# A SwiGLU kernel whose first 128 tokens of x are loaded by two queues, 64 rows each

## The chip, the cores and the metric

The kernel runs on one core of one Trainium2 chip. The metric is the device time of one execution in microseconds (us). Five engines of the core take part, each with its own queue of instructions that it works off in order: TensorE (PE in the profile, with its weight loads listed apart as PEld), VectorE (DVE), ScalarE (ACT), GpSimd (POOL) and SyncE (SP). SyncE and ScalarE also issue DMAs; a DMA issued on SyncE is told as queue q1 in the profile, one issued on ScalarE as q10. They meet through semaphores: a DMA adds 16 to its semaphore when all of its data has landed, and an engine that needs the data waits for that count.

## The reference

The kernel computes a feed-forward block with a SiLU gate, on x of 1 x 2048 x 512, with a hidden width F of 1376, all in bfloat16:

```python
def reference(x, w_gate, w_up, w_down):
    g = _silu(x @ w_gate)     # x: 2048 x 512, w_gate: 512 x 1376
    u = x @ w_up              # w_up: 512 x 1376
    return (g * u) @ w_down   # w_down: 1376 x 512
```

## The kernel before

**Tiling.** The 2048 tokens are worked in four chunks of 512 (`SC`), F in ten full tiles of 128 and a rest of 96. The inner dimension 512 is cut in `KD` = 4 pieces of 128. For chunk c and tile ft a group G (gate) and a group U (up) each run four matmuls of 128 x 128 weights against x transposed (`xT_sb`), and leave their result in one of eight PSUM banks. ScalarE applies SiLU to G, VectorE multiplies with U into `hT_sb`. When all of that is done the second half of the kernel multiplies `hT_sb` with `w_down` and stores the rows.

**How x gets transposed.** From the third tile of 128 tokens on, DMAs do it (`load_x`, line 93). The first two tiles (`NXN` = 2) come in untransposed by plain DMAs into `xn_sb` (`load_xn`, line 113; tile i has the semaphore `xn0` or `xn1`), and TensorE transposes them: `transposes(i)` (line 362) waits for the tile's load and then does four transposing matmuls, one for each dk, against the identity `ident`. Each leaves one 128 x 128 block in a bank; VectorE copies blocks dk = 0 and 2 to `xT_sb`, ScalarE dk = 1 and 3 (the loop at line 214). The matmuls of G and U wait for the copy that they read (`gu_step`, line 339).

**The order at the start, on each queue.**
- SyncE (`loads_on_sync`, line 123) issues in this order: xn0; the up weights of tile 0 (semaphore `wu0`); gate and up weights of tile 1 (`wg1`, `wu1`); gate and up weights of tiles 2 and 3 (`wg2`, `wu2`, twice as large); the transposing loads x0b and x0c of tokens 256 to 511; then the other weights, the other chunks of x, and `w_down`.
- ScalarE (`loads_on_scalar`, line 119) issues the gate weights of tile 0 (`wg0`) and then xn1. After that come the load of its function table and a small SiLU on a constant (line 277), and then its copies out of the banks.
- TensorE (from line 358) runs `N_WARM` = 5 matmuls of 512 columns and `N_FILL` = 2 of 128 on constants; then transposes(0), which waits for xn0; two more constant matmuls (`N_GAP`); G of tile 0 on tokens 0 to 127, which waits for `wg0` and for the copies; transposes(1), which waits for xn1; U of tile 0 on tokens 0 to 127, which waits for `wu0`; both groups on tokens 128 to 255; then, on tokens 0 to 255, G and U of tile 1 (`wg1`, `wu1`), G of tiles 2 and 3 (`wg2`), U of tiles 2 and 3 (`wu2`); then the same groups on the other half of the chunk (x0b, x0c). From there every group runs whole, 512 columns wide.

All waits for loads on TensorE go through `need(name, count)` (line 306), which waits until the semaphore is at 16 times the count.

Of the kernel before, what the change touches and what calls it, by code (L numbers as in the profile page):

```python
# [14 lines left out]
def bass_standalone__swiglu_ffn__prompt_kernel(nc, x, w_gate, w_up, w_down, out):  # L15
    _, S, D = x.shape
    F = w_gate.shape[1]
    P = 128
# [23 lines left out]
    xf = x[0]  # L42
# [8 lines left out]
    with ExitStack() as es:  # L51
# [19 lines left out]
        xn_sb = sb("xn_sb", [P, NXN, D], BF16)  # L71
# [10 lines left out]
        loads = {}  # L82

        def load_sem(name):
            loads[name] = sem(f"s_{name}")
            return loads[name]
# [6 lines left out]
        def load_x(eng, name, t0, t1):  # L93
            eng.dma_start_transpose(
                xT_sb[:, :, t0:t1], xf[t0:t1, :]
            ).then_inc(load_sem(name), 16)

        def load_w(eng, name, src, base, f0, f1):
            eng.dma_start(
                w_sb[:, :, base + f0:base + f1],  # L100
                src[:, f0:f1].rearrange("(k p) f -> p k f", p=P),
            ).then_inc(load_sem(name), 16)
# [4 lines left out]
        def load_gate(eng, a, b):  # L107
            load_w(eng, f"wg{a}", w_gate, 0, a * P, min(b * P, F))

        def load_up(eng, a, b):  # L110
            load_w(eng, f"wu{a}", w_up, UPH, a * P, min(b * P, F - 32))

        def load_xn(eng, i):
            eng.dma_start(xn_sb[:, i, :], xf[i * P:(i + 1) * P, :]).then_inc(load_sem(f"xn{i}"), 16)

        def out_rows(t):
            return of[t * P:(t + 1) * P, :]

        def loads_on_scalar(act):
            load_gate(act, *slabs[0])  # L120
            load_xn(act, 1)

        def loads_on_sync(sp):
            load_xn(sp, 0)
            load_up(sp, *slabs[0])
            for a, b in slabs[1:3]:
                load_gate(sp, a, b)
                load_up(sp, a, b)
            load_x(sp, "x0b", HT, HT + P)
            load_x(sp, "x0c", HT + P, SC)  # L130
            for a, b in slabs[3:]:
                load_gate(sp, a, b)
                load_up(sp, a, b)
            load_w(sp, "wut", w_up, F - (F - 32), F - 32, F)
            for c in range(1, NSC):
                load_x(sp, f"x{c}", c * SC, (c + 1) * SC)
            sp.dma_start(
                wd_sb[:, 0:NFF, :], w_down[0:NFF * P, :].rearrange("(k p) d -> p k d", p=P)
            ).then_inc(load_sem("wd"), 16)
            load_sem("wdt")  # L140
            for y0 in (0, 64):
                sp.dma_start(wd_sb[y0:y0 + 64, T01, :], w_down[NFF * P:F - SR, :]).then_inc(loads["wdt"], 16)
            for x0 in range(0, P, SR):
                sp.dma_start(wd_sb[x0:x0 + SR, T2, :], w_down[F - SR:F, :]).then_inc(loads["wdt"], 16)
            sp.dma_start(wd_sb[0:F_LAST, TAIL, :], w_down[NFF * P:F, :]).then_inc(load_sem("wdl"), 16)
# [19 lines left out]
        def tview(i, dk):  # L165
            return banks[KD * i + dk][:, 0:P // 2].bitcast(BF16)
# [47 lines left out]
        for i in range(NXN):  # L214
            for dk in range(KD):
                eng = "DA"[dk % 2]
# [16 lines left out]
        for at, t in enumerate(tiles):  # L233
            ob = at % NOS
            need = 16 * n_store[ob]
            parts = [(0, D)] if at < NST - 1 else [(0, LASTA), (LASTA, LASTB), (LASTB, D)]
            for c0, c1 in parts:
                g = add_group("O", t=t, c0=c0, c1=c1)
                eng = "A" if at % 2 == 1 and c0 == 0 else "D"
                op = add_op(  # L240
                    eng, g, kind="copy", out=o_sb[ob][:, c0:c1], src=g["bank"][:, 0:c1 - c0],
# [17 lines left out]
        def on_sync(sp):  # L259
            loads_on_sync(sp)  # L260
            store_tiles(sp, "S")
            for i in range(NOS):
                sp.wait_ge(s_out[i], 16 * n_store[i])
# [11 lines left out]
        def on_scalar(act):  # L275
            loads_on_scalar(act)
            act.activation(adummy[:, 0:4], zero_c, ACT.Silu)  # L277
            for op in act_ops:
                act.wait_ge(*ready(op))
                if op["kind"] == "silu":  # L280
                    if op["free"]:
                        act.wait_ge(s_D, op["free"])
                    fn = ACT.Silu
                else:
                    if op["stored"][1]:
                        act.wait_ge(*op["stored"])
                    fn = ACT.Copy
                act.activation(op["out"], op["src"], fn).then_inc(s_A, 1)  # L288
            store_tiles(act, "A")
# [13 lines left out]
        def on_tensor(pe):  # L303
            landed = set()

            def need(name, count=1):
                if name not in landed:
                    pe.wait_ge(loads[name], 16 * count)
                    landed.add(name)
# [50 lines left out]
            pe.wait_ge(s_I, 1)  # L360

            def transposes(i):
                need(f"xn{i}")
                for dk in range(KD):
                    pe.matmul(  # L365
                        tview(i, dk), lhsT=xn_sb[:, i, dk * P:(dk + 1) * P], rhs=ident[:, :],
                        start=True, stop=True, is_transpose=True,
                    ).then_inc(s_X, 1)

            first = groups[0:NB]  # L370
            transposes(0)
            warm(N_GAP, P)
            gu_matmuls(first[0], 0, P)
            transposes(1)
            gu_matmuls(first[1], 0, P)
            for dk in range(KD):
# [143 lines left out]
```

## Time and profile before

| | |
|---|---|
| median of 3 runs | 119.98 us (119.94 to 120.01) |
| the profiled execution's own time | 119.89 us |
| its span in the profile | 118.6 us |
| what lies around the span | 1.29 us |
| TensorE busy | 115.9 us, 98% of the span |
| VectorE / ScalarE busy | 38.0 us (32%) / 35.1 us (30%) |
| granted TensorE clock | 1.0 over the whole span |
| HBM read / written | 4.75 MB / 2.10 MB |

The span is what the profile covers, from the first instruction to the last; the time of a run has 1.29 us more in it. All times of single instructions below are counted from the span's start. A busy TensorE is not a TensorE at its peak: matmuls overlap, and their recorded ends are modelled. So for TensorE the start times of matmuls and weight loads say more than the busy time: in the stretches without a wait, a matmul with 128 columns starts every 0.056 us, one with 256 every 0.109 us and one with 512 every 0.216 us.

### The profile page before, as it was taken

Reading aid. Unit: us, or ns where it says so; the run is one execution under the profiler, and the core shown is the slowest. Engines: PE = TensorE matmul, PEld = TensorE weight load, DVE = VectorE, ACT = ScalarE, POOL = GpSimd, SP = SyncE. Lnnn points to the kernel's source line nnn. Section 1 sums busy time; section 2 is a strip of 40 time slices with the busy share of each in tenths; the row PEclk is TensorE's granted clock in tenths of the full one; section 3 lists DMA queues with packets and bytes.
Section 4 is the critical chain, followed back from the end, with each engine's and each line's share of the span. In section 5 each row is a group of like instructions: output and inputs, shape, how many; then the busy total and the mean of one; then the engine's idle time right before and its main releaser. Section 6 shows DMA issues by size and latency. Waiting matters only on the chain.

```text
span 118.6 us, 2344 instructions
## 1 busy us (share of the span) xinstructions
PE 115.9 (98%) x1019; PEld 59.7 (50%) x1019; DVE 38.0 (32%) x60; ACT 35.1 (30%) x62; POOL 1.1 (1%) x7
## 2 busy tenths in 40 slices
PE   7999999999999999999999999999999999999993
PEld 2788444444444444444444444444444445885442
DVE  0206542444433444324444244360000044003321
ACT  3407334353244272343263432330000033003021
POOL 1000000000000000000000000010000000000000
PEclk9999999999999999999999999999999999999999
DMA  3999999991000000000000000000000017200612
GB/s 87 290 186 336 296 161 221 268 357 25 0 6 0 0 0 0 0 3 3 0 0 6 0 0 0 0 0 6 0 6 0 0 57 237 70 0 6 202 64 88
DMA packets 17642, 8.83 MB, mean 74 GB/s; under 512 B 10624, under 2 KB 17632, under 8 KB 17632
## 3 DMA queue, kind: packets, MB, share of 16 engines
q1 hardware_dynamic: 16816, 8.33, 27.3%
q10 hardware_dynamic: 816, 0.36, 1.1%
q8 instruction: 8, 0.13, 0.5%
q14 instruction: 2, 0.02, 0.0%
HBM read 4.75 MB, written 2.10 MB: 58 GB/s over the span
## 4 chain that ended last, share of the span: by engine, by line
PE 98%; DVE 0%; issue 0%
PE bank L324 62%; PE bank L442 25%; PE bank L481 7%; PE bank L356 2%; PE bank L404 2%; PE bank L365 1%; DVE o_sb L300 0%
## 5 line engine op out<-in xcount | busy, mean ns | idle before, releaser
L324 PE MATMUL bank<-xT_sb,w_sb 128*128 128x512 bf16 (+2 forms) x384 | 73.3, 352 | 0.1
L324 PEld LDWEIGHTS bank<-xT_sb,w_sb 128*128 128x128 bf16 x384 | 36.2, 98 | 36.8 <-DMA w_sb<-in_w_gate_dram 0.3
L296 DVE TENSOR_TENSOR hT_sb<-sg_sb,bank 128x512 bf16<-128x512 f32 x40 | 27.5, 688 | 40.2 <-PE bank L324 39.3
L288 ACT ACTIVATE sg_sb<-bank 128x512 f32<-128x512 f32 x40 | 23.9, 597 | 40.6 <-PE bank L324 40.5
L442 PE MATMUL bank<-wd_sb,hT_sb 32*128 32x512 bf16 x496 | 29.0, 374 | 0.0
L442 PEld LDWEIGHTS bank<-wd_sb,hT_sb 32*128 32x128 bf16 x496 | 15.2, 93 | 11.6 <-issue 0.4
L300 DVE CAST o_sb<-bank 128x512 bf16<-128x512 f32 (+1 forms) x10 | 5.7, 595 | 31.1 <-PE bank L442 25.9
L288 ACT ACTIVATE o_sb<-bank 128x512 bf16<-128x512 f32 (+1 forms) x8 | 4.3, 582 | 33.6 <-PE bank L442 27.9
L481 PE MATMUL bank<-wd_sb,hT_sb 128*128 128x512 bf16 (+2 forms) x56 | 8.1, 304 | 0.0
L481 PEld LDWEIGHTS bank<-wd_sb,hT_sb 128*128 128x128 bf16 x56 | 4.2, 98 | 4.2 <-issue 0.4
L442 PE MATMUL bank<-wd_sb,hy_sb 32*128 32x512 bf16 (+1 forms) x32 | 5.0, 371 | 0.0
L296 DVE TENSOR_TENSOR hx_sb<-sgx_sb,bank 32x512 bf16<-32x512 f32 x4 | 2.8, 692 | 3.5 <-ACT sgx_sb L288 3.5
L288 ACT ACTIVATE sgx_sb<-bank 32x512 f32<-32x512 f32 x4 | 2.4, 588 | 4.5 <-PE bank L324 4.5
L356 PE MATMUL bank<-const-bfloat16-1.0 128*128 128x512 bf16 (+1 forms) x9 | 2.8, 463 | 0.8 <-PEq L505 0.8
L442 PE MATMUL bank<-wd_sb,hx_sb 32*128 32x512 bf16 (+1 forms) x16 | 3.0, 371 | 0.0
L288 ACT ACTIVATE sgy_sb<-bank 64x512 f32<-64x512 f32 x4 | 2.4, 590 | 0.1
L356 PEld LDWEIGHTS bank<-const-bfloat16-1.0 128*128 128x128 bf16 x9 | 1.0, 128 | 2.2 <-issue 2.2
L300 DVE COPY xT_sb<-bank 128x128 bf16<-128x128 bf16 x4 | 0.8, 222 | 4.3 <-PE bank L365 4.3
L404 PE MATMUL bank<-xT_sb,w_sb 128*64 128x512 bf16 x16 | 1.9, 382 | 0.0
L442 PEld LDWEIGHTS bank<-wd_sb,hy_sb 32*128 32x128 bf16 x32 | 1.6, 93 | 0.6
L277 ACT ACT_TABLE_LOAD x1 | 1.3, 1283 | 1.9 <-issue 1.9
L404 PEld LDWEIGHTS bank<-xT_sb,w_sb 128*64 128x64 bf16 x16 | 0.8, 109 | 1.0 <-DVE hT_sb L296 0.4
(15 smaller groups left out, 6.6 us busy)
## 6 DMA issues: line engine op xcount, KB each, us to landing
out_dram<-o_sb SPq DMA_DIRECT2D x15, 128.0 KB, 1.8
wd_sb<-in_w_down_dram SPq DMA_DIRECT2D x1, 1280.0 KB, 7.3
w_sb<-in_w_gate_dram SPq DMA_DIRECT2D x1, 480.0 KB, 5.5
w_sb<-in_w_up_dram SPq DMA_DIRECT2D x1, 448.0 KB, 6.2
w_sb<-in_w_gate_dram SPq DMA_DIRECT2D x1, 384.0 KB, 4.3
w_sb<-in_w_up_dram SPq DMA_DIRECT2D x1, 384.0 KB, 4.7
w_sb<-in_w_up_dram SPq DMA_DIRECT2D x2, 128.0 KB, 3.2
w_sb<-in_w_gate_dram SPq DMA_DIRECT2D x1, 256.0 KB, 3.6
```

Source lines behind the costliest of these rows:

```text
L277: act.activation(adummy[:, 0:4], zero_c, ACT.Silu)
L288: act.activation(op["out"], op["src"], fn).then_inc(s_A, 1)
L296: ins = dve.tensor_tensor(op["out"], op["a"], op["b"], ALU.mult)
L300: ins = dve.tensor_copy(op["out"], op["src"])
L324: return pe.matmul(bank[:, n0:n1], lhsT=w_sb[:, dk, col:col + P], rhs=xT_sb[:, dk, c * SC + n0:c * SC + n1], start=(dk == 0), stop=(dk == ...
L356: pe.matmul(banks[NB - 1][:, 0:width], lhsT=ones_w, rhs=ones_m[:, 0:width], start=True, stop=True)
L365: pe.matmul(tview(i, dk), lhsT=xn_sb[:, i, dk * P:(dk + 1) * P], rhs=ident[:, :], start=True, stop=True, is_transpose=True,).then_inc(s_X, 1)
L404: ins = pe.matmul(g["bank"][y0:y1, :], lhsT=w_sb[:, dk, YC0:YC0 + 64], rhs=xT_sb[:, dk, c * SC:(c + 1) * SC], start=(dk == 0), stop=(dk == ...
L442: ins = pe.matmul(g["bank"][:, 0:c1 - c0], lhsT=h, rhs=wd_sb[r0:r0 + SR, w, c0:c1], start=(start and fk == fks[0]), stop=(stop and fk == f ...
L481: ins = pe.matmul(g["bank"][:, 0:c1 - c0], lhsT=h, rhs=w, start=(last and fk == 0), stop=(fk == (NFF if last else NFF - 1)), skip_group_ch ...
```

## The change

The load of the first tile of x is cut in two DMAs of 64 rows each. The first half stays where it was, first on SyncE. The second half is issued on ScalarE, ahead of `wg0` and xn1. Both add to the same semaphore, so transposes(0) now waits for a count of 32 in place of 16 (`2 - i` is 2 for tile 0 and 1 for tile 1). `load_xn` gets the rows as arguments and makes the semaphore only on the first of the two calls. Nothing else is changed.

```diff
--- before.py
+++ after.py
@@ -110,18 +110,20 @@
         def load_up(eng, a, b):
             load_w(eng, f"wu{a}", w_up, UPH, a * P, min(b * P, F - 32))
 
-        def load_xn(eng, i):
-            eng.dma_start(xn_sb[:, i, :], xf[i * P:(i + 1) * P, :]).then_inc(load_sem(f"xn{i}"), 16)
+        def load_xn(eng, i, r0=0, r1=P):
+            s = loads[f"xn{i}"] if f"xn{i}" in loads else load_sem(f"xn{i}")
+            eng.dma_start(xn_sb[r0:r1, i, :], xf[i * P + r0:i * P + r1, :]).then_inc(s, 16)
 
         def out_rows(t):
             return of[t * P:(t + 1) * P, :]
 
         def loads_on_scalar(act):
+            load_xn(act, 0, P // 2, P)
             load_gate(act, *slabs[0])
             load_xn(act, 1)
 
         def loads_on_sync(sp):
-            load_xn(sp, 0)
+            load_xn(sp, 0, 0, P // 2)
             load_up(sp, *slabs[0])
             for a, b in slabs[1:3]:
                 load_gate(sp, a, b)
@@ -360,7 +362,7 @@
             pe.wait_ge(s_I, 1)
 
             def transposes(i):
-                need(f"xn{i}")
+                need(f"xn{i}", 2 - i)
                 for dk in range(KD):
                     pe.matmul(
                         tview(i, dk), lhsT=xn_sb[:, i, dk * P:(dk + 1) * P], rhs=ident[:, :],
```

## The prediction

> **What bounds the kernel now.** I read the chain of work that ended last first, since it says which engine's delays reach the end.
>
> ```profile
> PE 98%; DVE 0%; issue 0%
> PE bank L324 62%; PE bank L442 25%; PE bank L481 7%; PE bank L356 2%; PE bank L404 2%; PE bank L365 1%; DVE o_sb L300 0%
> ```
>
> TensorE is the chain, from the warm-up at L356 to the last tile. So the change is worth what it moves in TensorE's waits. It touches loads of the first microseconds, so next I read the weight loads in order of time, with the idle time before each and its cause in brackets.
>
> ```profile
> 2.93 0.15 PEld L356 LDWEIGHTS bank<-const-bfloat16-1.0 128*128 128x128 bf16 x1 [0.28 <-issue]
> 3.24 0.35 PEld L365 LDWEIGHTS bank<-ident,xn_sb 128*128 128x128 bf16 x4 [0.16 <-issue]
> 3.55 0.17 PEld L356 LDWEIGHTS bank<-const-bfloat16-1.0 128*128 128x128 bf16 x2
> 3.91 0.36 PEld L324 LDWEIGHTS bank<-xT_sb,w_sb 128*128 128x128 bf16 x4 [0.20 <-issue]
> 4.41 0.23 PEld L365 LDWEIGHTS bank<-ident,xn_sb 128*128 128x128 bf16 x4
> 4.59 1.58 PEld L324 LDWEIGHTS bank<-xT_sb,w_sb 128*128 128x128 bf16 x20
> 6.46 2.59 PEld L324 LDWEIGHTS bank<-xT_sb,w_sb 128*128 128x128 bf16 x31 [0.28 <-DMA w_sb<-in_w_gate_dram]
> ```
>
> The reader is to see four places: transposes(0) at 3.24, G of tile 0 at 3.91, transposes(1) at 4.41, and the one wait that the profile puts down to a DMA, for wg2, at 6.46. From 6.46 on matmuls start at their pace (every 0.109 us, later 0.216) without a hole through the rest of the first chunk. So what decides is when TensorE gets past 6.46; each us there is a us at the end.
>
> Then the issues of ScalarE and SyncE, and the transfers' time from issue to landing (last column).
>
> ```profile
> 0.81 0.47 ACTq L99 DMA_DIRECT2D w_sb<-in_w_gate_dram  x1
> 1.31 0.54 ACTq L114 DMA_DIRECT2D xn_sb<-in_x_dram  x1
> 1.87 1.28 ACT L277 ACT_TABLE_LOAD   x1 [1.87 <-issue]
> 3.17 0.20 ACT L277 ACTIVATE act_dummy<-const-float32-0.0 128x4 f32<-128x4 f32 x1
> 3.68 0.45 ACT L288 ACTIVATE xT_sb<-bank 128x128 bf16<-128x128 bf16 x2 [0.31 <-PE bank L365]
> ...
> 0.81 0.40 SPq L114 DMA_DIRECT2D xn_sb<-in_x_dram  x1
> 1.27 0.42 SPq L99 DMA_DIRECT2D w_sb<-in_w_up_dram  x1
> ```
> ```profile
> w_sb<-in_w_gate_dram SPq DMA_DIRECT2D x1, 256.0 KB, 3.6
> ...
> w_sb<-in_w_gate_dram ACTq DMA_DIRECT2D x1, 128.0 KB, 2.8
> xn_sb<-in_x_dram SPq DMA_DIRECT2D x1, 128.0 KB, 2.3
> xn_sb<-in_x_dram ACTq DMA_DIRECT2D x1, 128.0 KB, 3.1
> ```
>
> Issue plus this gives the landings, which the trace's landing records hold more finely: xn0 at 3.13, wg0 at 3.57, xn1 at 4.37, wg2 at 6.42 (and wu0 4.54, wg1 4.86, wu1 5.40, wu2 7.22). Set against the weight loads: transposes(0) waited for xn0, by at most 0.12 (the last warm-up matmul starts at 3.04, at its pace of 0.107 the next could at 3.15, it does at 3.27). G of tile 0 did not wait for wg0 but for the copies. Transposes(1) waited for xn1: the last matmul before starts at 4.18, at its pace of 0.056 the next could at 4.24, it does at 4.41, 0.17 lost. G of tile 2 lost 0.17 to wg2: 6.19 + 0.11 = 6.30 against 6.46.
>
> Last, how full the DMA engines are (the next to last number is the share of 16 engines):
>
> ```profile
> 2.20:2.40 0.20, 0.20 (x2) 0.03 (x1) 0.00 (x0) 0.20 (x1) 0.00 (x0) 1.00 0.60 192
> 2.40:2.60 0.20, 0.20 (x2) 0.09 (x1) 0.00 (x0) 0.20 (x1) 0.00 (x0) 1.00 1.04 288
> 3.00:3.50 0.50, 0.50 (x6) 0.34 (x5) 0.00 (x0) 0.36 (x2) 0.00 (x0) 1.00 1.17 310
> ```
>
> From 2.4 us on they have no room: what is put ahead of something delays it.
>
> **The change, part by part.**
>
> *SyncE's queue.* A DMA of 64 rows in place of 128, at the same place. Its issue isn't shorter: later on this queue loads of w_down with 32 rows and with 96 took 0.42 each. So wu0 and all behind it are issued as now. Cost 0.
>
> *ScalarE's queue.* One DMA issue is put ahead of everything. Start to start, SyncE's xn0 took 0.46, ScalarE's wg0 0.50 and xn1 0.56; I take 0.48. wg0 is issued at 1.29 in place of 0.81, xn1 at 1.79, the table load starts at 2.35 and ends at 3.63, the small SiLU ends at 3.85 (now 3.37). Today ScalarE then sits idle 0.31 until the transposes come; that cover is 0.18 short, and the two copies start at 3.86 in place of 3.68 and end at 4.31 (now 4.13). The matmul of dk = 3 in G of tile 0 goes from 4.18 to 4.36, and transposes(1) could start at 4.42. Today it starts at 4.41, because it waits for xn1. So this 0.18 lies beside xn1's wait and costs 0; if xn1 came early it would be 0.18 on the path.
>
> *xn0 sooner.* By today's wait a gain of 0 to 0.12 at transposes(0). VectorE's copies would profit, ScalarE's would not, since its table load is late now; and behind both stands xn1. I take 0.
>
> *The wait.* The same single instruction, with 32 in place of 16: 0.
>
> *wg0 and xn1 on the DMA engines.* This is the term that counts. The trace's packet records show wg0 as 32 packets of 256 B on each engine, 14 ns apart (0.46 us). On the engine that was last, xn0 ended at 2.78, wg0 at 3.24, then xn1, shared with wu0, at 3.98, 0.74 behind wg0, and its landing was 0.39 behind that. wg0 had the engines right behind xn0, because wu0 was issued 0.46 later. After the change wu0 (issued at 1.27) and wg0 (at 1.29) are level, both queued when xn0's two halves end. xn0's bytes are the same, so I leave their end at 2.78. If the two share the engines, or wu0 goes first, wg0 ends at 2.78 + 0.92 = 3.70, xn1 0.74 later at 4.44, and it lands at 4.83: 0.46 later than now. Bounds: 0, if wg0 is served first all the same. At the other end, wg0's first packet came 1.42 after its issue; with that, it is ready at 2.71, and engines that were through with xn0 at 2.23 may idle for part of the time until then, a loss that I put at up to 0.25 (half of the 0.48) for all that follows; then xn1 is 0.71 late. I take 0.46, since the late engines, which set a landing, are occupied until 2.78 in either case.
>
> wg0 itself lands at 4.03 then; G of tile 0 starts at some 4.07 in place of 3.91, but its second matmul has to wait for ScalarE's copy until 4.19 anyway. Hidden.
>
> *What the delay runs into.* TensorE's order behind transposes(1) is U, the second 128 columns, tile 1, then G of tile 2. Needs move 0.46 later with it (wu0 was needed at 4.60, wg1 at 5.42, wu1 at 5.86), and their landings at most 0.25; none becomes a wait. TensorE comes to wg2 at 6.30 + 0.46 = 6.76, where it has long landed (6.42, or 6.67 with the idle DMA time). Today's stall of 0.17 there is thus swallowed: cost 0.46 - 0.17 = **0.29**. Then wu2 (7.22, needed at 7.35 now, 7.64 then) and x0b (7.90 against 8.22 and 8.51) come in time.
>
> Sum: 119.89 + 0.29 = 120.18 against the profiled execution. The median of the runs is 0.09 above that execution, so **120.27**.
>
> A rule speaks against the change: the Trainium skill, "DMA: Bandwidth & Descriptors", section "Rules for kernel authors", says not to bother with splitting a transfer by halves of the partitions over two queues, as both spread over the same 16 engines. No row before shows two halves. By it the gain at transposes(0) is nothing, the sum is the one above, and rival three below has no source.
>
> **The rivals.**
>
> *One: hidden (not slower).* The arbitration of the engines gives ScalarE's queue wg0 before SyncE's wu0, and xn1 slips by no more than the 0.17 that today's wg2 stall gives back. The point is xn1's landing: up to 4.54 the time is unchanged, 119.98. For it: late engines today went to the other queue once xn0 was done. Against: now both queues have just delivered a half, and wu0 is issued first.
>
> *Two: worse.* The DMA engines idle while wg0 and wu0 are prepared, xn1 is 0.71 late: 0.71 - 0.17 = 0.54, 120.52. For it: wg0's first packet came 0.37 after xn0's, though issued together. Against: it takes the full bound on all engines.
>
> *Three: faster.* Four engines were held up 0.37 to 0.45 by one slow packet of xn0 each. If two queues overlap such reads, the halves end at 2.4, all loads gain some 0.38 and xn1 lands at 4.45; wg2 lands near 6.04, and the stall of 0.17 goes, with up to 0.12 from transposes(0): 119.69 to 119.81. For it: xn0's landings spread over 0.56 us, from 2.58 to 3.13. Against: ScalarE's late copies and xn1 lie between that gain and 6.46.
>
> That the halves land no sooner together (the change not doing what it says) has no time of its own: the gain is 0 in the sum already.
>
> **How the numbers follow.** Forecast 0.59, one 0.18, two 0.12, three 0.11. A measurement of this kernel can tell some 0.2% (0.24 us) from no change. The forecast's 0.29 with its bounds lies above 0.24 in about five parts of six: 0.50, with two 0.62 slower. Same: 0.09 from the forecast's low side, 0.18 from one and 0.03 from three, 0.30. Faster 0.08. The range takes in no change and the full bound: 119.90 to 120.60; the forecast's own is 120.15 to 120.45.
>
> **What would show it.** Right: wg0 landing at about 4.0 and xn1 at about 4.8; transposes(1) starting at about 4.87; ScalarE's first copy at about 3.86; no DMA wait at wg2, G of tile 2 starting near 6.75. Wrong: transposes(1) still near 4.4 and the wait for wg2 still there (rival one), or G of tile 2 before 6.4 (rival three), or a wait for wg2 that ends beyond 6.8 (rival two).

## The result and the profile after

The changed kernel takes 122.44 us (median of 6 runs, 120.86 to 122.71), the kernel before beside it 120.17 us (119.94 to 120.63). The ratio is 1.0139 with a 95% interval of 1.0102 to 1.0176: slower by about 1.4%. (The ratio leaves out the highest run, 122.71, which is also the profiled one; of the others 122.33, 122.56 and 122.63 are close to it, while 120.86 and 121.30 lie apart.) Forecast were 120.27 and at most 120.60.

The profiled execution took 122.71 us, with a span of 121.4 against 118.6: 2.8 us to account for. The chain of waits first:

```profile
PE 93%; DMA 3%; ACTq 1%; issue 1%; DVE 0%
PE bank L326 61%; PE bank L444 24%; PE bank L483 7%; DMA xn_sb<-in_x_dram 3%; PE bank L406 2%; ACTq L99 1%; PE bank L367 0%; ACTq L115 0%; DVE o_sb L302 0%
```

The chain no longer starts on TensorE's warm-up (L358 now). It starts with ScalarE's issues (L115 is the half of xn0 and xn1, L99 is wg0) and goes through the transfer of xn1 before it comes to TensorE. The weight loads in order of time show where TensorE stood:

```profile
2.93 0.15 PEld L358 LDWEIGHTS bank<-const-bfloat16-1.0 128*128 128x128 bf16 x1 [0.28 <-issue]
3.33 0.35 PEld L367 LDWEIGHTS bank<-ident,xn_sb 128*128 128x128 bf16 x4 [0.25 <-issue]
3.64 0.25 PEld L358 LDWEIGHTS bank<-const-bfloat16-1.0 128*128 128x128 bf16 x2
4.89 0.34 PEld L326 LDWEIGHTS bank<-xT_sb,w_sb 128*128 128x128 bf16 x4 [1.00 <-DMA w_sb<-in_w_gate_dram]
5.67 0.34 PEld L367 LDWEIGHTS bank<-ident,xn_sb 128*128 128x128 bf16 x4 [0.44 <-DMA xn_sb<-in_x_dram]
5.98 4.07 PEld L326 LDWEIGHTS bank<-xT_sb,w_sb 128*128 128x128 bf16 x28
```

Transposes(0) start 0.10 later than before, G of tile 0 at 4.89 in place of 3.91, now with a wait of 1.00 for wg0, and transposes(1) at 5.67 in place of 4.41, with a wait for xn1. The last line holds the surprise. Without any wait in it, 28 weight loads take 4.07 us; before, the line with 20 of them took 1.58. The matmuls by shape, between 4.6 and 9.4 us, say why (number, busy time, mean ns of one). The kernel before:

```profile
L324 PE MATMUL bank<-xT_sb,w_sb 128*128 128x256 bf16 x27 | 3.4, 273 | 0.0
L324 PE MATMUL bank<-xT_sb,w_sb 128*128 128x128 bf16 x28 | 2.0, 219 | 0.0
```

The changed kernel:

```profile
L326 PE MATMUL bank<-xT_sb,w_sb 128*128 128x256 bf16 x10 | 2.3, 414 | 0.0
L326 PE MATMUL bank<-xT_sb,w_sb 128*128 128x128 bf16 x16 | 2.1, 310 | 0.7 <-DMA w_sb<-in_w_gate_dram 0.7
```

Each matmul is longer, and in the records of single instructions they start 0.107 us (128 columns) and 0.213 us (256) apart, where before it was 0.056 and 0.109. TensorE ran at half its pace. It did so before too, but only up to 3.54; in the changed kernel up to 9.49. The views list a granted clock of 1.00 over the whole span for both kernels, and the table ahead of the prediction repeats it. The trace behind the views holds the clock's own record, which they do not print: its stretch of full clock begins at 3.55 in the kernel before and at 9.51 in the changed one, where the spacing halves.

The issues on the two queues:

```profile
0.82 0.59 ACTq L115 DMA_DIRECT2D xn_sb<-in_x_dram  x1
1.45 0.82 ACTq L99 DMA_DIRECT2D w_sb<-in_w_gate_dram  x1
2.30 0.53 ACTq L115 DMA_DIRECT2D xn_sb<-in_x_dram  x1
2.86 1.28 ACT L279 ACT_TABLE_LOAD   x1 [2.86 <-issue]
...
0.81 0.56 SPq L115 DMA_DIRECT2D xn_sb<-in_x_dram  x1
1.43 0.57 SPq L99 DMA_DIRECT2D w_sb<-in_w_up_dram  x1
```

and the time from issue to landing:

```profile
w_sb<-in_w_gate_dram SPq DMA_DIRECT2D x1, 256.0 KB, 3.9
...
w_sb<-in_w_gate_dram ACTq DMA_DIRECT2D x1, 128.0 KB, 3.4
...
xn_sb<-in_x_dram ACTq DMA_DIRECT2D x1, 128.0 KB, 3.3
...
xn_sb<-in_x_dram SPq DMA_DIRECT2D x1, 64.0 KB, 2.1
xn_sb<-in_x_dram ACTq DMA_DIRECT2D x1, 64.0 KB, 2.4
```

A DMA of 64 rows takes longer to issue (0.56 and 0.59) than one of 128 rows did (0.40), and wg0 behind it takes 0.82 in place of 0.47. By the landing records xn0 is whole at 3.23 (3.13 before), wg0 lands at 4.85 (3.57), xn1 at 5.63 (4.37), wg2 at 7.06 (6.42).

**The account of the 2.8 us**, from the start times of matmuls. Transposes(1) go from 4.42 to 5.68: 1.26 for the late xn1. From there to G of tile 2 it took 2.05 before, of which 0.17 was the wait for wg2, so 1.88 of work; now it takes 3.39 without that wait: 1.51 for the half pace, and 0.17 of the old wait swallowed. G of tile 2 starts at 9.07 (6.46 before), and the last few matmuls at half pace cost 0.21. 1.26 - 0.17 + 1.51 + 0.21 = 2.81.

### The profile page after: what moved, and what is told of

The parts are those of the page before. It is cut to its first block, busy times and chain, and to the rows that moved or that the text cites. A ratio compares the mean times of both kernels' runs of the same rounds, so it can differ in the third digit from the quotient of the medians.

```text
span 121.4 us, 2337 instructions
## 1 busy us (share of the span) xinstructions
PE 117.3 (97%) x1011; PEld 61.2 (50%) x1019; DVE 38.1 (31%) x60; ACT 35.0 (29%) x62; POOL 1.1 (1%) x7
## 4 chain that ended last, share of the span: by engine, by line
PE 93%; DMA 3%; ACTq 1%; issue 1%; DVE 0%
PE bank L326 61%; PE bank L444 24%; PE bank L483 7%; DMA xn_sb<-in_x_dram 3%; PE bank L406 2%; ACTq L99 1%; PE bank L367 0%; ACTq L115 0%; DVE o_sb L302 0%
## 5 line engine op out<-in xcount | busy, mean ns | idle before, releaser
L326 PE MATMUL bank<-xT_sb,w_sb 128*128 128x512 bf16 (+2 forms) x377 | 74.5, 360 | 1.1 <-DMA w_sb<-in_w_gate_dram 0.7
L326 PEld LDWEIGHTS bank<-xT_sb,w_sb 128*128 128x128 bf16 x384 | 37.5, 101 | 37.7 <-DMA w_sb<-in_w_gate_dram 1.0
L358 PE MATMUL bank<-const-bfloat16-1.0 128*128 128x512 bf16 (+1 forms) x9 | 2.9, 486 | 0.8 <-PEq L507 0.8
L358 PEld LDWEIGHTS bank<-const-bfloat16-1.0 128*128 128x128 bf16 x9 | 1.1, 139 | 2.2 <-issue 2.2
L367 PE MATMUL bank<-ident,xn_sb 128*128 128x128 bf16 x8 | 1.2, 302 | 0.2 <-DMA xn_sb<-in_x_dram 0.2
```

The lines of the kernel that those rows point to most:

```text
L326: return pe.matmul(bank[:, n0:n1], lhsT=w_sb[:, dk, col:col + P], rhs=xT_sb[:, dk, c * SC + n0:c * SC + n1], start=(dk == 0), stop=(dk == ...
L358: pe.matmul(banks[NB - 1][:, 0:width], lhsT=ones_w, rhs=ones_m[:, 0:width], start=True, stop=True)
L367: pe.matmul(tview(i, dk), lhsT=xn_sb[:, i, dk * P:(dk + 1) * P], rhs=ident[:, :], start=True, stop=True, is_transpose=True,).then_inc(s_X, 1)
```

## The experiments

Two questions: does the half pace cost time of its own, or would TensorE have waited anyway; and what makes wg0 and xn1 1.3 us late, when the change moves them by one issue?

**The hole filled.** 16 constant matmuls in place of 2 between transposes(0) and G of tile 0, in the changed kernel.

```diff
-N_GAP = 2
+N_GAP = 16
```

> The changed kernel, with 16 constant matmuls in place of 2 between transposes(0) and the first gate matmuls (they compute nothing that is kept). In the changed kernel TensorE stands idle from 3.85 to 4.90 us and then runs at half pace (0.107 us per matmul of 128 columns) up to 9.4. Theory 'clock': that hole came before TensorE had been busy long enough to get its full pace; with the hole filled the pace is 0.056 before the first gate matmul, only the late loads cost (transposes(1) at about 5.7 as xn1 lands at 5.63, G of tile 2 at about 7.56, 1.1 later than before), and the time is about 121.1 us (120.7 to 121.4) with little spread. Rival 'loads only': the late loads account for the whole loss and the half pace hides behind them; then the time stays at 122.4.

Measured: 121.22 us (121.08 to 121.49), ratio to before 1.0082 (1.0055 to 1.0108). Its weight loads (start, duration, count, wait):

```profile
3.70 1.12 PEld L358 LDWEIGHTS bank<-const-bfloat16-1.0 128*128 128x128 bf16 x16
5.28 0.23 PEld L326 LDWEIGHTS bank<-xT_sb,w_sb 128*128 128x128 bf16 x4 [0.46 <-DMA w_sb<-in_w_gate_dram]
5.87 0.23 PEld L367 LDWEIGHTS bank<-ident,xn_sb 128*128 128x128 bf16 x4 [0.36 <-DMA xn_sb<-in_x_dram]
```

The half pace ends at 4.01, among the fillers; from there on matmuls start 0.06 apart, and the trace's record of full clock begins at 4.00. wg0 and xn1 land even later than in the changed kernel (5.24 and 5.83), and yet the kernel is 1.2 us faster. The clock theory holds: with the pace saved, what is left is the late xn1, 5.87 - 4.42 - 0.17 = 1.28, against a difference of the spans of 119.9 - 118.6 = 1.3. The spread of the runs went from 1.85 us to 0.41. The holes of 0.46 and 0.36 that come after the full pace did not take it away.

**The warm-up left out**, in the kernel before. The loads are as before, nothing but TensorE's start is changed.

```diff
-N_WARM = 5
-N_FILL = 2
+N_WARM = 0
+N_FILL = 0
```

> The kernel before, without the seven warm-up matmuls ahead of transposes(0); all loads as before. Theory 'clock': landings stay (wg0 3.57, xn1 4.37, wg2 6.42), but TensorE runs at 0.107 us per 128 columns for some 3 us or more from 3.2 on, and the time rises by 0.7 to 2 us with a spread over the runs. Rival 'loads only': as the loads land when they did, 120.0 to 120.3.

Measured: 121.30 us (120.38 to 121.84, 10 runs), ratio 1.0066 (1.0034 to 1.0098). xn0, wg0 and xn1 land within 0.02 of before; TensorE is at half pace up to 6.30 in the profiled execution, one of the fastest (120.56). Loads in time and pace late: about 1 us, with a wide spread. In part the expectation missed: wg2 landed at 6.79, 0.37 later than in the trace of before. The warm-up need not be the reason: in the first of the two runs with more constant matmuls below, whose loads are those of before as well, wg2 landed at 6.73. The landings of the later loads differ by this much from one execution to the next; those of xn0, wg0 and xn1 agree within 0.1 in these three traces.

**The split alone**, both halves on SyncE, ScalarE as before.

```diff
         def loads_on_scalar(act):
-            load_xn(act, 0, P // 2, P)
             load_gate(act, *slabs[0])
...
             load_xn(sp, 0, 0, P // 2)
+            load_xn(sp, 0, P // 2, P)
```

> The split alone: both halves of xn0 issued on SyncE one after the other, ScalarE as before (wg0 first, then xn1). Theory 'one row' (DMAs of both queues are made ready one after the other, 0.25 to 0.5 us each): the order is half, wg0, half, then wu0 and xn1; wg0 lands about 3.4 to 3.6, xn0 is whole only at about 3.4 to 3.5 (3.13 before), xn1 about 0.3 later (4.7); transposes(0) starts 0.2 to 0.4 later, and the time is 120.3 to 121. Rival 'ScalarE's queue': only what is put ahead on ScalarE costs; wg0 and xn1 land as before and the time is within 0.2 of before.

Measured: 122.13 us (121.65 to 122.66), ratio 1.0155 (1.0105 to 1.0205). wg0 landed in time (3.43), xn1 too (4.10), but xn0 was whole only at 4.51:

```profile
4.62 0.35 PEld L367 LDWEIGHTS bank<-ident,xn_sb 128*128 128x128 bf16 x4 [1.54 <-issue]
```

Transposes(0) were 1.4 late (before: 3.24), far more than the 0.2 to 0.4 expected, and the full pace came at 9.33. Neither theory had the size: the first half's first packet came 1.78 after its issue, where the whole xn0 took 1.05, and the second half was issued after wg0 and xn1 (at 1.43). What it shows is that being late by this much at xn0 costs as much as at wg0.

**The additional DMA alone**: xn0 whole on SyncE, and on ScalarE 64 rows into a tile that nobody reads.

```diff
         def loads_on_scalar(act):
+            act.dma_start(spare[P // 2:P, :], xf[P // 2:P, :]).then_inc(load_sem("spare"), 16)
             load_gate(act, *slabs[0])
```

> No split: xn0 whole on SyncE as before, and on ScalarE an additional load of 64 rows into a spare tile that nobody reads, ahead of wg0. Theory 'one row': wg0 and xn1 are as late as in the changed kernel (about 4.8 and 5.6), xn0 lands at about 3.1 to 3.2, and the time is that of the changed kernel, 120.9 to 122.7. Rival 'ScalarE's queue alone', late by one issue: wg0 at about 4.1 and xn1 at 4.9, time about 120.3. Rival 'halves' (it is the two-queue split of xn0 that costs): within 0.2 of before.

Measured: 122.39 us (121.30 to 122.68), ratio 1.0159 (1.01 to 1.0218), the changed kernel's time. xn0 landed at 3.11, as before, wg0 at 5.17, xn1 at 5.84:

```profile
5.21 0.34 PEld L326 LDWEIGHTS bank<-xT_sb,w_sb 128*128 128x128 bf16 x4 [1.43 <-DMA w_sb<-in_w_gate_dram]
5.88 0.34 PEld L367 LDWEIGHTS bank<-ident,xn_sb 128*128 128x128 bf16 x4 [0.32 <-DMA xn_sb<-in_x_dram]
```

So the loss needs no split of xn0; a DMA put ahead of wg0 on ScalarE is enough. Theory 'one row' forecast this outcome, though wg0 came 0.4 later than it said.

**128 rows in place of 64 in that additional DMA, and the split by columns.** Is it the shape of 64 rows, slow to issue, that does it?

```diff
-            act.dma_start(spare[P // 2:P, :], xf[P // 2:P, :]).then_inc(load_sem("spare"), 16)
+            act.dma_start(spare[:, :], xf[0:P, :]).then_inc(load_sem("spare"), 16)
```

> As the run with an additional load ahead of wg0 on ScalarE, but the additional load has 128 rows (128 KB) in place of 64 (64 KB). Theory 'shape': a DMA of 64 rows is itself slow to issue and to make ready (0.55 to 0.59 us to issue on either queue, against 0.40 for 128 rows); with 128 rows the issue takes 0.40 to 0.47, wg0 is issued at about 1.3 and lands at about 4.0 to 4.3, and the loss is clearly smaller, 120.3 to 121.2, though twice the bytes are loaded. Theory 'any DMA': one more DMA ahead costs the same whatever its rows; wg0 lands at 4.8 or later and the time is 121.5 to 122.6.

```diff
-            eng.dma_start(xn_sb[r0:r1, i, :], xf[i * P + r0:i * P + r1, :]).then_inc(s, 16)
+            eng.dma_start(xn_sb[:, i, c0:c1], xf[i * P:(i + 1) * P, c0:c1]).then_inc(s, 16)
```

> The changed kernel with the cut made along the columns: each half has all 128 rows and 256 of the 512 columns. Theory 'shape': issue times 0.40 to 0.47, wg0 issued at about 1.3 and landed by about 4.0 to 4.3, time 120.3 to 121.2. Theory 'any DMA': as the changed kernel, wg0 at about 4.8 and 121 to 122.7.

Measured: the additional 128 rows 123.29 us (122.33 to 123.66), ratio 1.0244 (1.0196 to 1.0292); the split by columns 122.42 us (121.88 to 122.58), ratio 1.0176 (1.0145 to 1.0207). In both the issues were short again (0.40 and 0.41 for the first DMA on ScalarE, 0.47 for wg0), so wg0 was issued at 1.24, but it landed at 4.70 and 4.97. The shape theory falls: 64 rows are slower to issue, but wg0 is as late without that. The rival 'any DMA' held for the split by columns, and for the 128 additional rows it was off by 0.1 in wg0 and by 0.7 in the time.

**The two loads of ScalarE exchanged**, in the kernel before: no additional DMA, xn1 and then wg0.

```diff
         def loads_on_scalar(act):
-            load_gate(act, *slabs[0])
             load_xn(act, 1)
+            load_gate(act, *slabs[0])
```

> The kernel before with ScalarE's two loads in the other order, xn1 and then wg0; no additional DMA, xn0 whole. wg0 goes from second to fourth in the row of DMAs. Theory 'place in the row and clock': wg0 lands at about 4.5, G of tile 0 starts at about 4.6 after a hole of 0.7 on TensorE, and where that keeps the full pace from coming the time is 121 to 122; xn1 lands early, at about 3.7, and costs nothing. Rival 'the additional DMA': without one more DMA the loads in all come as before, and the time is 120 to 120.5.

Measured: 120.77 us (10 runs), ratio 1.0042 (1.0009 to 1.0075). The runs fall in two groups: seven from 120.40 to 121.15 and three from 121.97 to 122.36. The profiled execution is of the upper group, 122.21: xn0 at 3.59, as xn1's packets now ran beside its own (from 1.97 and 1.84), wg0 at 4.62, and half pace up to 9.12. In that execution the expectation holds but for xn0, whose delay left a hole of 0.41 in place of 0.7 ahead of G. The median lies between the two theories. So wg0 comes late behind another DMA even when none is added. That the lower group is that in which the full pace came early fits the 1.2 us of the filled hole, but no execution of it was traced.

**wg0 and wu0 exchanged between the queues**, in the changed kernel, so that wg0 is on SyncE, behind one half only.

```diff
-            load_gate(act, *slabs[0])
+            load_up(act, *slabs[0])
...
-            load_up(sp, *slabs[0])
+            load_gate(sp, *slabs[0])
```

> The changed kernel with wg0 and wu0 exchanged: SyncE half of xn0, then wg0; ScalarE half of xn0, then wu0, then xn1. The additional DMA stays, wg0 moves from fourth to third place. Theory 'place in the row': wg0 lands at about 4.2 to 4.5 (4.85 in the changed kernel), xn1 still at about 5.6; the hole on TensorE ahead of G of tile 0 shrinks from 1.04 to 0.4 to 0.7; the late xn1 still costs about 1.1, so 121.2 where the full pace comes in time and up to 122.4 where not; median 121.2 to 122.2. Rival 'total': the same 122.4 as the changed kernel.

Measured: 122.89 us (121.29 to 123.34), ratio 1.0166 (1.0107 to 1.0225). wg0 landed at 5.14 (wu0 at 5.50), later than in the changed kernel, though its first packet came at 2.68 already (3.21 there). An earlier place in the row did not help; the rival's 122.4 was nearer.

**Both weight loads of tile 0 on ScalarE**, xn1 on SyncE, in the changed kernel.

```diff
             load_gate(act, *slabs[0])
-            load_xn(act, 1)
+            load_up(act, *slabs[0])
...
             load_xn(sp, 0, 0, P // 2)
-            load_up(sp, *slabs[0])
+            load_xn(sp, 1)
```

> The changed kernel with both weight loads of tile 0 on one queue: SyncE issues half of xn0, then xn1; ScalarE half of xn0, then wg0, then wu0. The additional DMA and its place ahead of wg0 stay; what goes is that wu0 on SyncE and wg0 on ScalarE are fetched side by side, and that xn1 is third on ScalarE. Theory 'side by side': the DMA engines keep above 270 GB/s from 2.6 to 4.2 us (163 to 190 in much of that stretch in the changed kernel), wg0 lands at 4.0 to 4.3 and xn1 at 4.0 to 4.5; TensorE's hole ahead of G of tile 0 is under 0.5, and the time is 120.2 to 121. Theory 'any DMA ahead': wg0 lands at 4.7 or later and the time is 121.3 to 122.6, even with xn1 early.

Measured: 122.25 us (120.96, 121.49, 123.00, 123.01) beside 120.47. xn1 landed early, at 3.66, but wg0 at 5.58:

```profile
3.49 0.34 PEld L367 LDWEIGHTS bank<-ident,xn_sb 128*128 128x128 bf16 x4 [0.41 <-issue]
3.79 0.25 PEld L358 LDWEIGHTS bank<-const-bfloat16-1.0 128*128 128x128 bf16 x2
5.62 0.23 PEld L326 LDWEIGHTS bank<-xT_sb,w_sb 128*128 128x128 bf16 x4 [1.58 <-DMA w_sb<-in_w_gate_dram]
```

The theory of two weight loads side by side falls; 'any DMA ahead' had all of this. In this execution (121.49) the four weight loads ahead of the hole took 0.34, half pace, with matmuls 0.107 apart up to the last at 4.00; the four behind it took 0.23, full pace. The trace's record of full clock begins at 4.55, inside the hole of 1.58. So a hole ahead of the full pace doesn't always forfeit it: TensorE's work stopped at about 4.11 here and at about 3.96 in the changed kernel, and there the full clock came only at 9.51.

Set side by side, the traces hold one plain rule for wg0. In all eight with another DMA ahead of it on its queue it landed at 4.62 or later, in the six where it is first on its queue by 3.64.

What goes slow behind the additional DMA can be seen, though not why. The share of the DMA engines and GB/s (last two numbers), the kernel before:

```profile
2.60:3.00 0.40, 0.40 (x3) 0.12 (x2) 0.00 (x0) 0.40 (x1) 0.00 (x0) 1.00 1.23 279
3.00:3.40 0.40, 0.40 (x5) 0.24 (x4) 0.00 (x0) 0.36 (x2) 0.00 (x0) 1.00 1.19 306
3.40:3.80 0.40, 0.40 (x6) 0.31 (x4) 0.23 (x2) 0.12 (x1) 0.00 (x0) 1.00 1.16 336
```

and the changed kernel:

```profile
2.60:3.00 0.40, 0.40 (x3) 0.12 (x2) 0.00 (x0) 0.14 (x1) 0.00 (x0) 1.00 0.75 168
3.00:3.40 0.40, 0.39 (x4) 0.15 (x3) 0.00 (x0) 0.40 (x1) 0.00 (x0) 1.00 0.78 167
3.40:3.80 0.40, 0.40 (x5) 0.40 (x6) 0.13 (x1) 0.40 (x1) 0.00 (x0) 1.00 1.03 187
```

The rate is little more than half. Every traced kernel with a DMA of 64 rows at the start has such a stretch (its lowest rate over 0.4 us between 3.0 and 4.2 is 109 to 167 GB/s). With 128 additional rows it stays at 286 to 297 between 3.0 and 3.8, and wg0 is late all the same, with twice the bytes ahead of it. Split by columns it is 257 and 208 there, but 166 from 2.6 to 3.0; and the last kernel below, with no such DMA, falls to 161 from 4.2 to 4.6. That the 64 rows cause the low rate is not shown. The order of landing changed too: before it was xn0, wg0, xn1, wu0, wg1; in the changed kernel xn0, wu0, wg0, wg1, xn1.

**Attempts at a faster version.** xn1 and wu0 exchanged between the queues, in the kernel before:

```diff
-            load_xn(act, 1)
+            load_up(act, *slabs[0])
...
-            load_up(sp, *slabs[0])
+            load_xn(sp, 1)
```

> The kernel before with xn1 and wu0 exchanged between the queues: SyncE issues xn0, xn1, then wg1 and so on, ScalarE wg0, wu0. No additional DMA. xn1 should land at about 3.9 to 4.1 in place of 4.37, and transposes(1) start at about 4.25 in place of 4.41. As the wait for wg2 at 6.46 stands, theory 'wg2 bounds' says the time stays within 0.2 of before; if wg2 lands sooner, up to 0.17 faster.

Measured: 120.30 us, ratio 0.9998 (0.9976 to 1.0021). xn1 at 3.94 as expected, wg2 at 6.49, no gain.

More constant matmuls, in the kernel before and in the one just told:

```diff
-N_FILL = 2
-N_GAP = 2
+N_FILL = 3
+N_GAP = 6
```

> The kernel before with 3 in place of 2 short constant matmuls ahead of transposes(0) and 6 in place of 2 behind it, so that TensorE has almost no hole up to G of tile 0 (before: 0.12 and 0.22 us). Loads unchanged. Theory 'clock': the full pace comes by about 3.6 in every run, fewer runs above 120.3, median 119.9 to 120.1, up to 0.3 faster than before; where the full pace is late, the four more matmuls at 0.107 cost up to 0.3. Theory 'loads only': 120.3 or up to 0.2 slower.

> As the run before it, with xn1 and wu0 exchanged between the queues (SyncE xn0, xn1; ScalarE wg0, wu0). xn1 lands at 3.94, so TensorE comes to wg2 some 0.17 earlier and waits there. Theory 'clock': full pace by 3.6 where the exchange alone had it only at 5.4; median 119.8 to 120.1. Theory 'loads only': 120.3, as the exchange alone.

Measured: ratios 1.0004 (0.9986 to 1.0023) and 1.0009 (0.9987 to 1.0031): no difference. In their profiled executions full pace came at 3.58 (before: 3.54) and at 4.52 (with the exchange alone: 5.43), so the clock theory's 3.6 held in the first alone, and its gain in neither. In the first TensorE waited 0.15 for wg1 and 0.41 for wg2, which landed at 6.73; one execution of each can't tell whether the filling moved the pace. No version beat the kernel before.

## Why the prediction was wrong

- **What bounds the kernel: right.** TensorE's waits at the start decide, and xn1's wait was the one of the loads that counted.
- **xn0 sooner, 0: right in counting no gain.** It came 0.10 later. The Trainium skill's rule in "DMA: Bandwidth & Descriptors", "Rules for kernel authors", against splitting by halves is borne out: whole at 3.23 against 3.13.
- **ScalarE's queue, 0.48 later: mis-sized.** The issue of wg0 began 0.64 later (0.81 to 1.45) and ended 0.99 later (1.28 to 2.27); xn1 and the table load came 0.99 later. The price of a DMA with 64 rows was read from the loads of w_down with 32 and 96 rows; those with 64 in the same place had taken 0.68 and 0.87 in the trace of before, and one of those with 32 had taken 0.58, and I passed them over.
- **wg0 and xn1 on the DMA engines, 0.46: the first step that failed.** It measured 1.28 for wg0 and 1.26 for xn1. Of wg0's 1.28, 0.64 is the later start of its issue, 0.33 a longer way from there to its first packet (1.76 in place of 1.42), and 0.31 the transfer and its landing. The 0.33 is the longer issue itself (0.82 in place of 0.47): from the end of the issue to the first packet it took 0.94, and 0.96 before. "The late engines, which set a landing, are occupied until 2.78 in either case" took wg0 to be ready by then; its first packet came at 3.21. The stated bound of 0.71 took the latency from the start of the issue to the first packet as fixed. It was not. Nor do the issues explain it all: split by columns, wg0's issue began 0.44 later and took 0.47, and it landed 1.40 late.
- **wg0 hidden behind ScalarE's copies: wrong.** G of tile 0 started at 4.90, 0.05 behind wg0's landing; the copies were through at 4.69.
- **What the delay runs into, 1:1: the step that failed worst.** I let everything behind transposes(1) move with it at unchanged pace. The trace of before held the sign: 0.107 us between matmuls up to 3.54, 0.056 from there. I used both numbers as the pace at their places and did not ask what turns one into the other. By the Trainium skill, "TensorE: Matmul & The Clock Gate", Part 1, the array runs at half clock until it has been busy for a stretch of about 3.4 us, and the window in which this is counted runs freely, so that it comes at different points in different runs. The trace agrees in kind: in the kernel before TensorE was busy from 0.84, with short holes, and got the full pace 2.7 us on, at 3.55; the filled kernel got it at 4.01; the changed one stopped at 3.96, waited 1 us, and got it at 9.5. The stretch of full clock on record lasts 116.05 us in the five traces where it begins at 3.55 to 4.55, and 112.64 in the seven where it begins at 9.12 to 10.22: 3.41 apart, and nothing between. The spread of the changed kernel's runs is what one would see if some of them got it in time; that was not traced.
- **The rivals.** Rival two (xn1 0.71 late) had the right direction, and its 120.52 was still 0.34 under the fastest run. None had a change of TensorE's pace in it.

With xn1's true 1.26 the prediction's own sum gives 1.26 - 0.17 = 1.09, which is near what the filled kernel showed (121.22 - 120.32 = 0.90 by the medians, 1.3 by the spans); the other 1.2 us of the median is the pace.

What stays open: why wg0's own issue takes 0.82 behind a DMA of 64 rows, why wg0 lands late behind any other DMA even when its issue is short, and why the DMA engines run at little more than half their rate for a us. The theories that gave a reason (the shape, the place in the row, two weight loads side by side, ScalarE's queue alone) failed; the rival that any DMA ahead makes wg0 late held, and it gives none.

## What to carry to other kernels

While TensorE is still at half pace, a wait can cost more than its length: here the late loads cost about 1 us by themselves, and the half pace behind the hole 1.2 us more. So check in the trace from which matmul on the spacing halves, and hold any wait for a load that would fall ahead of it against that point. Expect the runs to differ, since a hole of 1 us kept the pace away in the execution traced here, and one of 1.58 in another kernel's did not. Constant matmuls that bridge the wait are a cheap insurance when a load must be late. And one more small DMA at the head of a queue delays the loads behind it by much more than its own issue time; measure that before counting on the earlier arrival of half a tile.

## What the runs showed of the hardware that was not expected

- The granted clock that the profile's views list stays at 1.00 over the whole span in every kernel here, also where TensorE runs at half pace up to 9.5 us. The spacing of the matmuls shows it, and so does the trace's own record of the clock (3.55 us before, 9.51 in the changed kernel), which two of the 14 traces lack.
- A DMA of 64 rows of 1 KB took 0.55 to 0.59 us to issue on either queue, one of 128 rows of 1 KB 0.39 to 0.41 at the same place, and one of 128 rows of 512 B 0.40 to 0.41.
- The full clock came inside a hole: on record from 4.55 us, while TensorE had no work from about 4.11 to 5.62, and the matmuls behind the hole ran at full pace. In the filled kernel it outlasted holes of 0.46 and 0.36 us.
